# Reordering the first batch of an attention-plus-SwiGLU kernel: quarters of k and v, early dummy products, split copies, narrow first weights

## Chip, cores, metric

One core of one Trainium2 chip. The metric is device time in microseconds, the median of several executions. Other kernels were always timed beside runs of the kernel before, in the same rounds on the same chip. All runs quoted are of the fast state, and every run gave correct results.

A word on the spread: executions of the kernel before lie between 580.8 and 583.1 us, one at 584.2. The trace's span is some 1.8 us shorter than the time (581.1 for 582.86).

## The reference

```python
k_proj = einsum('ks,bhsd->bhkd', E, k)          # E, F: 64 x 1024
v_proj = einsum('ks,bhsd->bhkd', F, v)          # q, k, v: 8 x 8 x 1024 x 64
attn   = softmax(q @ k_proj^T / 8)              # over 64 columns
x      = (attn @ v_proj) -> (8192, 512)
out    = (silu(x @ w_gate) * (x @ w_val)) @ w_out   # 512 -> 1536 -> 512
```

Inputs and output are float32; the kernel computes in bf16 with float32 sums.

## The kernel before

The kernel is one long stream of products for 16 chunks of 512 tokens: gate, value, then output, with the attention of the next batches placed between them. Only batch 0 has no stream to hide in. These are the parts of its start that the argument touches:

```python
def u_KV(b, what="kv", hs=(0, H), at="a"):      # project heads hs of k and/or v
    t = ...one PSUM bank, [128, 8, 64] f32...
    for j in range(8):                           # 8 products per call and operand
        matmul(out=t[lo:lo+64, h0:h1], lhsT=w[:, j], rhs=src[b][:, h0:h1, j], ...)
    if "k" in what: scalar.copy(ks[:, h0:h1], t[0:64, h0:h1])
    if "v" in what: vector.tensor_copy(BDV[0:64, ps, 0:64], ...); vector.tensor_copy(BDV[64:128, ps, 64:128], ...)

def u_KT(b, at="a"):                             # transpose k', spread it into block-diagonal BD
    ...4 transposes into one PSUM tile...
    for c in range(2):
        vector.tensor_copy(bd[0:64, :, c, 0:64], src)
        copy(scalar if b else vector, bd[64:128, :, c, 64:128], src)

# ... batch 0, in program order (cut):
turn(0); warm(4)                                 # E transposed; 4 dummy products
for h in range(7): cast_k(gpsimd if h == 3 else vector, h)
load_q(0, 0, 2); load_v(0, 2); load_w_gv(0); load_w_gv(1)     # 4 blocks of 128 columns
u_KV(0, "k", (0, 4), at="y"); warm(2)
cast_k(scalar, 7)
u_KV(0, "k", (4, 8), at="y")
turn(1)                                          # F transposed
u_KT(0, at="v")
# u_T: q transposed; u_S: scores and exp; u_R, u_N: row sums, scaling; u_A: A transposed; u_PV: A v'
u_T x4 and u_S x4
for u in range(3): u_R(0, u); u_N(0, u)
u_KV(0, "v", (0, 4), at="y"); u_R(0, 3); u_N(0, 3)
u_A(0, 0); warm(2); u_A(0, 1); u_KV(0, "v", (4, 8), at="y"); u_A(0, 2)
u_PV x2; u_A(0, 3); u_PV x2                      # then the stream: f_g, f_v, ...
```

The softmax here doesn't subtract the row's maximum and nothing guards it: scores larger than these inputs give would overflow.

## Time and profile before

| | before |
|---|---|
| median time | 581.71 us (580.81 to 582.29, 4 runs) |
| profiled run | 582.86 us, span 581.1 |
| TensorE busy | 98% |
| first scores / first value group begin | 16.68 / 26.52 us |
| span from there on | 554.56 us |

In a timeline line stand: start in us, duration, engine, source line, operation, written and read tiles, count, and in brackets how long the engine had been idle and what released it. "kvp" are the projections, "sc" the scores, "aTp" the transposes of A, "pv" A times v', "gps" and "vps" gate and value products. "PEld" are weight loads. BD and BDV are k' and v' spread into block-diagonal tiles; PSUM is the memory that TensorE writes its sums to, in banks. The beginning of the first value group is the marker of what follows. A warning on the clock column: it averages the records of the granted clock, and before the first record it says 1.00 although the durations show half speed. The profiled run of the kernel before has a mean of 1.000 although its first record comes at 20.92 us. I read the first rise from durations and from the time of that record.

### The profile page before, as it was taken

To read this page: it belongs to the slowest core of one execution; us is meant where nothing else is said; L and a number is where in the kernel's file an instruction comes from. 1 tells how busy PE (TensorE), PEld (TensorE's weight loads), DVE (VectorE), ACT (ScalarE), POOL (GpSimd) and SP (SyncE) were. 2 spreads that over 40 slices of the span, in tenths; PEclk is the share of its full clock that TensorE was granted. 3 is DMA by queue.
4 is the path that set the end of the run, shared out by engine and by line. 5 is a ranking of instruction groups with operands and counts; after the bars stand their busy time and mean duration, and the time that the engine had idled before them with its cause. 6 is when DMAs were issued, how large, how long until landed. Compare 5 with 4: busy or idle time off the path is not lost.

```text
span 581.1 us, 7901 instructions
## 1 busy us (share of the span) xinstructions
PE 567.6 (98%) x2952; PEld 268.1 (46%) x2952; DVE 337.7 (58%) x576; ACT 242.4 (42%) x428; POOL 106.8 (18%) x119
## 2 busy tenths in 40 slices
PE   5999999999999999999999999999999999999997
PEld 3644444544444444444444444444444444444443
DVE  2787564766556664666546764566555674545550
ACT  2545435454435434354345434354343533443321
POOL 5625040224102320025001240022300220000000
PEclk9999999999999999999999999999999999999999
DMA  9999955309930399016980289313990124001012
GB/s 223 190 200 192 205 87 100 73 19 170 203 81 37 80 194 179 37 45 110 177 159 29 63 145 197 74 38 77 183 193 37 38 55 73 37 36 37 19 37 91
DMA packets 100599, 61.34 MB, mean 106 GB/s; under 512 B 51792, under 2 KB 91216, under 8 KB 100560
## 3 DMA queue, kind: packets, MB, share of 16 engines
q0 software_dynamic: 40176, 28.84, 34.3%
q1 hardware_dynamic: 60384, 31.99, 23.9%
q8 instruction: 23, 0.38, 0.3%
q14 instruction: 16, 0.13, 0.1%
HBM read 60.29 MB, written 16.78 MB: 133 GB/s over the span
## 4 chain that ended last, share of the span: by engine, by line
PE 94%; ACT 2%; DVE 2%; DMA 1%; issue 0%; SPq 0%; DVEq 0%; ACTq 0%
PE yps L344 28%; PE vps L318 28%; PE gps L303 28%; PE kvp L150 3%; PE sc L229 3%; PE pv L287 2%; DMA kraw<-in_k_dram 1%; DVE hT L332 1%; PE qTp L195 1%; PE aTp L276 1%; ACT qT L138 0%; DVE s L327 0%; DVE zz L244 0%; PE kTp L174 0%; ACT ysb L353 0%
## 5 line engine op out<-in xcount | busy, mean ns | idle before, releaser
L327 DVE SCALAR_TENSOR_TENSOR s<-th,gps 128x512 f32<-128x512 f32 x192 | 130.5, 680 | 136.1 <-ACT th L311 135.8
L303 PE MATMUL gps<-xT,wg 128*128 128x512 bf16 x768 | 197.9, 379 | 0.5 <-ACT xT L138 0.3
L318 PE MATMUL vps<-xT,wv 128*128 128x512 bf16 x768 | 197.2, 379 | 0.0
L344 PE MATMUL yps<-wo,hT 128*128 128x512 bf16 x768 | 194.6, 379 | 0.7 <-ACT ysb L353 0.7
L311 ACT ACTIVATE th<-gps 128x512 f32<-128x512 f32 x192 | 114.7, 597 | 154.4 <-PE gps L303 152.7
L332 DVE TENSOR_TENSOR hT<-s,vps 128x512 bf16<-128x512 f32 x192 | 132.0, 688 | 22.8 <-PE vps L318 2.5
L344 PEld LDWEIGHTS <-hT 128*128 128x128 bf16 x768 | 75.1, 98 | 91.5 <-issue 1.0
L318 PEld LDWEIGHTS <-wv 128*128 128x128 bf16 x768 | 72.9, 98 | 83.4 <-issue 4.0
L303 PEld LDWEIGHTS <-wg 128*128 128x128 bf16 x768 | 73.1, 98 | 81.9 <-issue 1.0
L260 POOL TENSOR_TENSOR AAd<-ee,rr 128x512 bf16<-128x512 f32 x48 | 49.9, 1040 | 300.6 <-issue 165.3
L353 ACT ACTIVATE ysb<-yps 128x512 f32<-128x512 f32 x64 | 38.2, 597 | 76.0 <-PE yps L344 76.0
L138 ACT CAST xT<-pv 128x512 bf16<-128x512 f32 x61 | 35.4, 584 | 50.4 <-PE pv L287 50.4
L244 DVE TENSOR_REDUCE zz<-ee 128x8 f32<-128x512 f32 x64 | 43.5, 680 | 20.0 <-ACT ee L233 19.7
L233 ACT ACTIVATE ee<-sc 128x512 f32<-128x512 f32 x64 | 38.0, 597 | 20.0 <-PE sc L229 18.8
L260 POOL TENSOR_TENSOR AA<-ee,rr 128x512 bf16<-128x512 f32 x15 | 15.5, 1040 | 63.7 <-DVE rr L246 25.8
L287 PE MATMUL pv<-AT,BDV 128*128 128x512 bf16 x64 | 23.6, 379 | 0.9 <-ACT AT L138 0.7
L229 PEld LDWEIGHTS <-qTd 128*128 128x128 bf16 x192 | 14.8, 98 | 11.3
L150 PE MATMUL kvp<-kb,ET 128*64 128x512 bf16 (+1 forms) x72 | 17.1, 389 | 1.7 <-POOL kb L138 1.0
L229 PE MATMUL sc<-BD,qTd 128*128 128x128 bf16 x192 | 18.6, 219 | 0.0
L246 DVE RECIPROCAL rr<-zz 128x8 f32<-128x8 f32 x64 | 13.0, 203 | 6.3
L164 DVE CAST BDV<-kvp 64x256 bf16<-64x256 f32 (+1 forms) x9 | 3.6, 396 | 22.3 <-ACT ks L160 20.0
L150 PE MATMUL kvp<-vb,FT 128*64 128x512 bf16 (+1 forms) x72 | 16.4, 375 | 0.0
(50 smaller groups left out, 157.1 us busy)
## 6 DMA issues: line engine op xcount, KB each, us to landing
out_dram<-ysb SPq DMA_DIRECT2D x64, 256.0 KB, 2.3
qb<-in_q_dram POOLq DMA_DIRECT2D x15, 512.0 KB, 17.2
kb<-in_k_dram POOLq DMA_DIRECT2D x7, 1024.0 KB, 11.5
vb<-in_v_dram POOLq DMA_DIRECT2D x7, 1024.0 KB, 14.0
kraw<-in_k_dram SPq DMA_DIRECT2D x4, 512.0 KB, 6.0
wg<-in_moe_w_gate_dram POOLq DMA_DIRECT2D x6, 256.0 KB, 10.2
wv<-in_moe_w_val_dram POOLq DMA_DIRECT2D x6, 256.0 KB, 10.7
wo<-in_moe_w_out_dram POOLq DMA_DIRECT2D x2, 768.0 KB, 15.4
```

The lines of the kernel that those rows point to most:

```text
L150: nc.tensor.matmul(out=t[lo : lo + 64, h0:h1].rearrange("p h d -> p (h d)"), lhsT=w[:, j, :], rhs=src[b][:, h0:h1, j, :], start=(j == 0), ...
L229: nc.tensor.matmul(out=ps[:, n, :], lhsT=t[:, n, :], rhs=BD[b % 2][:, 4 * g + n, :], start=True, stop=True)
L233: nc.scalar.activation(out=e[:].rearrange("p h j k -> p (h j k)"), in_=ps[:].rearrange("p a k -> p (a k)"), func=AF.Exp, scale=scale,)
L244: nc.vector.reduce_sum(out=z[:], in_=e[:], axis=AX.X)
L260: eng.tensor_tensor(out=a.rearrange("p j h k -> p h j k"), in0=ee.pop((b, u))[:], in1=rr.pop((b, u))[:].unsqueeze(3).to_broadcast([P, 4, 2 ...
L303: nc.tensor.matmul(out=ps[:], lhsT=wg[:, kt, f * P : (f + 1) * P], rhs=x[:, kt, :], start=(kt == 0), stop=(kt == NKT - 1),)
L311: nc.scalar.activation(out=th[:], in_=ps[:], func=AF.Tanh, scale=0.5)
L318: nc.tensor.matmul(out=ps[:], lhsT=wv[:, kt, f * P : (f + 1) * P], rhs=x[:, kt, :], start=(kt == 0), stop=(kt == NKT - 1),)
L327: nc.vector.scalar_tensor_tensor(out=s1[:], in0=th[:], scalar=1.0, in1=g[:], op0=ALU.add, op1=ALU.mult)
L332: nc.vector.tensor_tensor(out=hT[c][:, f, :], in0=s1[:], in1=ps[:], op=ALU.mult)
L344: nc.tensor.matmul(out=yy[c][:], lhsT=hT[c][:, f, i * P : (i + 1) * P], rhs=wo[:, f, :], start=(f == 0), stop=(f == NFT - 1),)
L353: nc.scalar.activation(out=ysb[:], in_=yy.pop(c)[:], func=AF.Copy, scale=0.5)
```

## The change

The intent: start the stream sooner. Project k and v by quarters as they land, cast k on three engines, turn k' in two halves with its copies split over VectorE and ScalarE, let dummy products open TensorE's clock from the beginning, take F's turn out of the way of the scores, begin row sums early, and load only one block of 128 weight columns ahead of the softmax.

```diff
-            nc.vector.tensor_copy(out=BDV[b % 2][0:64, ps, 0:64], in_=tv[:, ps, 0, :])
+            copy(nc.vector if b else nc.scalar, BDV[b % 2][0:64, ps, 0:64], tv[:, ps, 0, :])
...                                   # u_KT, now for prs=(0, 2) and (2, 4)
-            copy(nc.scalar if b else nc.vector, bd[64:128, :, c, 64:128], src)
+            nc.scalar.copy(out=bd[64:128, slice(*prs), c, 64:128], in_=src)
...
-        nc.sync.dma_start(out=ef[1][:], in_=F)
+        zeros = const.tile([P, CW], BF16, name="zeros"); nc.vector.memset(zeros[:], 0.0)
...
+        warm(8)
         turn(0)
-        warm(4)
-        for h in range(7): cast_k(nc.gpsimd if h == 3 else nc.vector, h)
+        warm(6)
+        cast_k(nc.vector, 0); cast_k(nc.gpsimd, 1)
         load_q(0, 0, 2)
-        load_v(0, 2); load_w_gv(0); load_w_gv(1)
+        load_v(0, (0, 4, 6, 8)); load_w_gv(0, 1)
+        cast_k(nc.vector, 2); cast_k(nc.scalar, 3)
+        nc.scalar.dma_start(out=ef[1][:], in_=F)
+        u_KV(0, "k", (0, 2), at="y"); u_KV(0, "k", (2, 4), at="y")
+        cast_k(nc.vector, 4); cast_k(nc.scalar, 5)
+        warm(2)
+        u_KV(0, "k", (4, 6), at="y"); u_KT(0, at="v", prs=(0, 2))
+        cast_k(nc.vector, 6); cast_k(nc.scalar, 7)
+        warm(2)
+        u_KV(0, "k", (6, 8), at="y"); u_KT(0, at="v", prs=(2, 4))
...                                   # T0, T1, S0, S1, R0, N0, then turn(1), T2, T3, ...
+        load_w_gv(1, 2) ... load_k(1)            # the other loads, behind the row scaling
+        warm(3)
+        u_A(0, 0, nc.scalar); u_A(0, 1, nc.scalar); u_KV(0, "v", (0, 4), at="y"); u_A(0, 2, nc.scalar)
+        u_PV(0, 0, 0, nc.vector); u_A(0, 3, nc.vector); u_PV(0, 0, 1, nc.scalar)
+        u_KV(0, "v", (4, 6), at="y"); u_PV(0, 0, 2, nc.vector)
+        u_KV(0, "v", (6, 8), at="y"); u_PV(0, 0, 3, nc.scalar)
```

## The prediction

> **What bounds the kernel now.** I read the page first, then busy times by stretch, then the timeline of the start, then the DMA view.
>
> ```profile
> PE 567.6 (98%) x2952; PEld 268.1 (46%) x2952; DVE 337.7 (58%) x576; ACT 242.4 (42%) x428; POOL 106.8 (18%) x119
> PE   5999999999999999999999999999999999999997
> ```
>
> TensorE bounds the span; only the first and last slices (14.5 us each) are not full. By stretch (length, then PE, PEld, DVE, ACT, POOL busy, clock, DMA share, GB/s):
>
> ```profile
> 0.00:5.00 5.00, 0.42 (x4) 0.45 (x5) 1.51 (x4) 1.28 (x1) 1.14 (x8) 1.00 0.58 161
> ...
> 100.00:560.00 460.00, 460.00 (x2352) 214.41 (x2350) 273.41 (x457) 194.01 (x341) 71.52 (x72) 1.00 0.50 92
> ```
>
> From 100 to 560 us PE is never idle. The change touches only the first batch, so its worth is how much sooner the dense stream of gate and value products begins. The timeline shows that start, with its waits:
>
> ```profile
> 4.58 1.11 PE L431 MATMUL efp<-ident_fp,Eraw 64*128 64x64 f32 x8 [4.58 <-DMA Eraw<-in_E_dram]
> ...
> 11.47 0.62 ACT L138 CAST kb<-kraw 128x512 bf16<-128x512 f32 x1 [0.63 <-DMA kraw<-in_k_dram]
> ...
> 12.14 1.87 PE L150 MATMUL kvp<-kb,ET 128*64 128x256 bf16 x8 [0.73 <-ACT kb L138]
> ...
> 13.94 1.14 PE L431 MATMUL efp<-ident_fp,Fraw 64*128 64x64 f32 x8
> ...
> 16.42 0.29 DVE L138 COPY BD<-kTp 64x256 bf16<-64x256 bf16 x1
> ...
> 16.68 0.61 PE L229 MATMUL sc<-BD,qT 128*128 128x128 bf16 x4
> ...
> 18.93 1.92 PE L150 MATMUL kvp<-vb,FT 128*64 128x256 bf16 x8
> ...
> 21.81 1.06 PE L150 MATMUL kvp<-vb,FT 128*64 128x256 bf16 x8
> ...
> 24.93 0.59 PE L287 MATMUL pv<-AT,BDV 128*128 128x512 bf16 x2 [0.67 <-ACT AT L138]
> ...
> 26.52 1.02 PE L318 MATMUL vps<-xT,wv 128*128 128x512 bf16 x4
> ```
>
> The first value group starts at 26.52; that is my marker. The path to it: last k quarter lands at 11.4; cast; eight products (1.87); F's eight transposes (1.1); k' transposed; four copies of k' into BD one after another on DVE (15.50 to 16.71); scores from 16.68; softmax, A transposes, PV; marker. Two stretches, then: 16.68 to the scores, 9.84 from there.
>
> The DMA view of the first 13 us:
>
> ```profile
> GB/s 0 0 0 0 0 0 151 252 233 239 290 183 208 384 384 391 372 347 359 372 391 391 384 403 397 391 378 422 378 120 107 77 93 176 195 191 173 183 189 180
> kraw<-in_k_dram SPq DMA_DIRECT2D x4, 512.0 KB, 6.0
> qb<-in_q_dram POOLq DMA_DIRECT2D x2, 256.0 KB, 4.9
> ```
>
> k streams at 370 to 400 GB/s until about 9.5, then a hole of some 1.5 us before q and v flow, because POOL issued q only at 8.47, after its cast of head 3. (Casting transfers are counted by the bytes written, so 190 there is some 380 read.) Dividing the same view into single issues gives landings of k at 5.7, 7.6, 8.9 and 11.4, q 13.2 and 14.5, v 18.2 and 20.7, first weights 22.0 and 23.4. All land before they are used, so in the second stretch no transfer is the bound.
>
> **What the Trainium skill says.** "TensorE: Matmul & The Clock Gate", Part 1: the array runs at half clock until it has been busy through a free-running window of about 3.4 us. The trace agrees: eight like products took 1.92 us at 18.93 and 1.06 at 21.81, so TensorE was cold for 20 us, its gaps breaking every window. "Perfetto Trace Analysis", DVE / Act Engine Instruction: the sequencer pushes an instruction into a wait queue and fetches the next. So F's DMA, though written after a cast on ACT, may be issued early. ACT issues no DMA here, so this trace can't show it. "DMA: Bandwidth & Descriptors", Specifications: line rate needs 512 bytes or more. The new 128-column weights are written as 256-byte rows; no row here shows their rate.
>
> **The change part by part.**
>
> (1) Dummies from a zero tile. A DVE memset of this size takes 0.27 (the BDV ones); DVE starts at 0.91, so PE starts near 1.25 instead of 4.58. Eight cold products at 0.43 (two took 1.04 with overlap, four 1.86) run to 4.7, E's turn to 5.8, six more to 7.5 or 8.4. Some 6 us are dense, so a full window fits and the clock should be full by about 8. The dummies lie in dead time: first casts end at 6.4.
>
> (2) k by quarters, casts shared by DVE, ACT and POOL. A quarter is eight products of 128 columns: 1.87/2 = 0.94 cold, about 0.5 warm. But ACT now does four things in strict order: cast 3, ks copies, cast 5, ks copy, two BD copies, cast 7. With 0.62 per cast and 0.25 (estimate, from 0.36 for double the size) per small copy: cast 3 at 7.6 to 8.25, two ks to 9.0, cast 5 to 9.9 (k at 8.9, slowed by F and q), products, ks to 10.75, BD copies to 11.3, cast 7 to 11.9 or 12.1. So it is no earlier than now, when it ends at 12.09. After it: products 0.5 (saves 1.4), ks 0.3, no F turn (saves 1.1), k' transposes 0.3, half of the BD copies on two engines 0.5 (saves 0.7). With q in place (two qT copies, 0.6 side by side) scores start near 14.1 instead of 16.68: 2.6 gained.
>
> (3) Second stretch, from scores at 14.1. ACT: exp 0, 1 to 15.65; F's half 0.4; qT 2, 3 to 17.2 (0.58 each, both now on ACT and behind the exps); exp 2, 3 to 18.35. Now all four exps ended 3.08 after the first scores; then 4.25. Row sums: N0 on POOL 16.0 to 17.05, N1 to 18.25, N2 18.7 to 19.75, N3 on DVE 19.55 to 20.25. A0, A1, v(0:4) are done by 19.75; A2 to 20.1; BDV copy on DVE behind N3 to 20.55; PV0 20.6; xT0 on DVE 20.95 to 21.65; A3's copy on DVE behind it to 22.1; v(4:6) and its copies to 22.3; PV2 22.35, xT2 to 23.4; v(6:8) 22.6 to 23.1, copies to 23.6; PV3 23.65; xT3 on ACT 24.05 to 24.65; last gate product 24.7; value group near 24.9. That is 10.8 against 9.84: 1.0 given back.
>
> (4) Loads. POOL is free after one cast at 6.55, so q goes out 1.9 us earlier and the hole fills; v should land by 18. The 128-column pair is in by 20 or 21. The next pairs go out behind N2, from 19.8, landing from about 24 on; each column block of 128 needs 0.52 MB at 380 GB/s = 1.4 us against 1.73 us of products, so the stream keeps ahead. Nothing on the path.
>
> Sum: 2.6 - 1.0 = 1.6 us; 581.7 - 1.6 = 580.1.
>
> **Rivals.**
> (a) The clock stays cold, because F32 transposes or gaps break the window again. For: it was cold through 20 us that the page calls nearly all busy. Quarters then cost 0.94 and every later PE step doubles; I estimate 1 to 1.3 us back: 581.2.
> (b) The k path isn't held by casts but by landing. With POOL and ACT issuing q and F into k's stream, the last quarter could land at 12 or later, and nearly half of the front gain goes: 580.9. Against: by 8.4 nearly all of k has moved.
> (c) The tail isn't as serial as I laid it: with warm products and DVE and ACT both free, the second stretch takes 9 us as the author meant, marker at 23, 578.2. Against: xT0, A3 and N3 share DVE, and PV2 stands ahead of v(6:8) in PE's order.
> (d) Weights come late, since three of the first four 128-column blocks are now issued behind the softmax instead of ahead of it: a stall of 1 to 2 us around 26 to 29 eats the gain: 581.7. Against: the margins in (4) are over 1 us.
>
> **Range and chances.** The path from 1.25 to 24.9 is some forty steps, each uncertain by some 0.1, with two open switches (clock, landing), and repeats of before spread over 1.5 us. I put 8 in 10 on 578.2 to 581.5, centre 580.1. Even a marker at 17 would not give 11.6 us, and the start can't lose that, so within 2% is all but sure: 0.98, with 0.01 each side.
>
> **What would show it.** Right: PE busy from about 1.3; the eight v products in about 1 us instead of 1.92; scores near 14; first value group near 25; same length from there to the end; PE busy without waits on weights. Step 2 is wrong if cast 7 waits for k rather than for ACT's order; step 3 is wrong if the marker comes less than 10 us after the first scores, or more than 11.5; the whole is wrong if the time moves without the marker moving.

## The result, and the profile after

The changed kernel took 586.46 us (586.03 to 587.28, 4 runs) against 581.71: slower by 0.85 per cent. Ratios are the mean time of one kernel's fast runs over the mean of the other's of the same rounds, so not quite the ratio of the medians; here 1.0085, 95% interval 1.0067 to 1.0103.

The page of the changed kernel, busy times, then TensorE by slice of 14.6 us and its granted clock:

```profile
PE 571.6 (98%) x2989; PEld 268.9 (46%) x2989; DVE 336.6 (58%) x575; ACT 245.3 (42%) x438; POOL 108.7 (19%) x122
PE   7799999999999999999999999999999999999997
PEclk9799999999999999999999999999999999999999
```

The second slice has a clock of 7 tenths: something new. The timeline of the start, the lines that answer to those shown of before:

```profile
1.19 3.59 PE L442 MATMUL warm<-zeros 128*128 128x512 bf16 x8 [1.19 <-DVE zeros L414]
...
7.72 0.62 ACT L137 CAST kb<-kraw 128x512 bf16<-128x512 f32 x1 [1.90 <-DMA kraw<-in_k_dram]
...
7.73 0.54 ACTq L458 DMA_DIRECT2D Fraw<-in_F_dram  x1
...
14.33 0.61 PE L149 MATMUL kvp<-kb,ET 128*64 128x128 bf16 x8 [1.25 <-ACT kb L137]
...
17.24 1.03 PE L228 MATMUL sc<-BD,qT 128*128 128x128 bf16 x8 [1.21 <-ACT qT L137]
...
30.10 1.02 PE L317 MATMUL vps<-xT,wv 128*128 128x512 bf16 x4
```

First scores at 17.24 instead of 16.68; first value group at 30.10 instead of 26.52. After it the span goes on for 585.06 - 30.10 = 554.96 us, against 554.56. So nearly the whole loss lies ahead of the marker: 0.56 us up to the scores, 3.02 between scores and marker, 0.4 behind it.

What fills this time is in the chain of waits, followed back from the first value group of the changed kernel (start, us, what):

```profile
6.37 2.72 PE warm L442 x6
9.09 0.87 PE kvp L149 x8
...
9.98 0.27 ACT ks L159
...
10.29 0.62 PE kvp L149 x8
...
12.57 0.23 DVE BD L181
...
12.82 0.27 ACT BD L182
...
13.11 0.24 DVE BD L181
...
13.37 0.26 ACT BD L182
...
13.66 0.63 ACT kb L137
...
21.66 1.28 PE warm L442 x3
22.94 0.69 PE aTp L275 x8
...
24.66 0.27 ACT BDV L137
...
24.95 0.31 DVE BDV L137
```

Three things stand here that I had put beside the path. Dummies: six of them run until the first products of k, three until the A transposes. Products that wait for a copy: the second quarter waits until ScalarE has taken the first out of the same bank. And copies in turns: DVE, ACT, DVE, ACT, one after the other. Behind those four copies stands the cast of the last head, behind that the last quarter of k.

### The profile page after: what moved, and what is told of

It reads as the page before. It is cut to its first block, busy times and chain, and to the rows that moved or that the text cites. A ratio compares the mean times of both kernels' runs of the same rounds, so it can differ in the third digit from the quotient of the medians.

```text
span 585.1 us, 7989 instructions
## 1 busy us (share of the span) xinstructions
PE 571.6 (98%) x2989; PEld 268.9 (46%) x2989; DVE 336.6 (58%) x575; ACT 245.3 (42%) x438; POOL 108.7 (19%) x122
## 4 chain that ended last, share of the span: by engine, by line
PE 94%; ACT 2%; DVE 2%; issue 1%; DVEq 0%; ACTq 0%
PE yps L343 28%; PE vps L317 28%; PE gps L302 27%; PE kvp L149 3%; PE sc L228 3%; PE pv L286 2%; PE warm L442 1%; DVE hT L331 1%; ACT qT L137 1%; PE aTp L275 0%; PE efp L430 0%; PE qTp L194 0%; DVE s L326 0%; ACT BD L182 0%; DVE zz L243 0%
## 5 line engine op out<-in xcount | busy, mean ns | idle before, releaser
L259 POOL TENSOR_TENSOR AA<-ee,rr 128x512 bf16<-128x512 f32 x15 | 15.6, 1040 | 66.0 <-ACT th L310 27.7
L228 PEld LDWEIGHTS <-qTd 128*128 128x128 bf16 x192 | 14.7, 98 | 11.3
L137 DVE CAST BDV<-kvp 64x256 bf16<-64x256 f32 (+2 forms) x17 | 6.7, 396 | 22.9 <-ACT ks L159 20.0
L149 PE MATMUL kvp<-vb,FT 128*64 128x512 bf16 (+2 forms) x80 | 15.7, 339 | 0.0
## 6 DMA issues: line engine op xcount, KB each, us to landing
kb<-in_k_dram POOLq DMA_DIRECT2D x7, 1024.0 KB, 11.3
```

Of the source, the lines that this page charges most:

```text
L137: (nc.scalar.copy if eng is nc.scalar else eng.tensor_copy)(out=out, in_=in_)
L149: nc.tensor.matmul(out=t[lo : lo + 64, h0:h1].rearrange("p h d -> p (h d)"), lhsT=w[:, j, :], rhs=src[b][:, h0:h1, j, :], start=(j == 0), ...
L228: nc.tensor.matmul(out=ps[:, n, :], lhsT=t[:, n, :], rhs=BD[b % 2][:, 4 * g + n, :], start=True, stop=True)
L259: eng.tensor_tensor(out=a.rearrange("p j h k -> p h j k"), in0=ee.pop((b, u))[:], in1=rr.pop((b, u))[:].unsqueeze(3).to_broadcast([P, 4, 2 ...
```

## The experiments

Each line of the table is one kernel. First scores and first value group are from its profiled run and depend on when that run's clock rose, so only runs with the same rise are to be compared closely (changed, e3, e7: 9.6 to 9.7 us; e1, e8: 10.1 to 10.2; e4, e12, e13, e14: 5.4 to 5.9; the others 3.9 to 5.3). The clock is the range of the mean granted clock over the timed runs.

What the rise alone is worth can be read from e10 and e5, which have the instructions of the changed kernel up to the scores, but for the loads of weights (e10) and one more transposed part of q (e5). From the timeline of e10, whose clock rose at 5.1:

```profile
6.32 1.46 PE L442 MATMUL warm<-zeros 128*128 128x512 bf16 x6 [0.52 <-DVE ET L137]
...
12.72 0.61 PE L149 MATMUL kvp<-kb,ET 128*64 128x128 bf16 x8 [1.25 <-ACT kb L137]
...
15.64 1.03 PE L228 MATMUL sc<-BD,qT 128*128 128x128 bf16 x8 [1.21 <-ACT qT L137]
```

The scores begin at 15.64 in both, 1.60 us sooner than in the profiled run of the changed kernel: that much of its 17.24 is the late rise. How often its other runs rose late the record does not show. The profiled runs of e3 and e7, with the same late rise, were the slowest of theirs, so there the trace shows less than the median gained.

| kernel | median | before | ratio (95%) | scores | value group | clock |
|---|---|---|---|---|---|---|
| changed | 586.46 | 581.71 | 1.0085 (1.0067-1.0103) | 17.24 | 30.10 | 0.993-0.994 |
| e1 fewer dummies | 585.62 | 581.92 | 1.0062 (1.0049-1.0074) | 15.60 | 27.62 | 0.987-0.999 |
| e2 one engine per tile | 585.22 | 581.92 | 1.0057 (1.0043-1.0071) | 14.41 | 27.85 | 0.993-1.000 |
| e3 v ahead | 584.81 | 581.92 | 1.0047 (1.0034-1.0061) | 17.27 | 29.26 | 0.993-0.994 |
| e4 before + dummies | 581.78 | 581.92 | 1.0000 (0.9988-1.0013) | 15.25 | 25.28 | 0.994-1.000 |
| e5 second stretch as before | 584.66 | 582.25 | 1.0042 (1.0026-1.0059) | 15.64 | 26.13 | 0.991-0.997 |
| e6 casts ahead | 584.50 | 582.25 | 1.0044 (1.0030-1.0059) | 14.75 | 26.31 | 0.994-1.000 |
| e7 gaps filled | 583.95 | 582.25 | 1.0038 (1.0026-1.0050) | 17.20 | 28.75 | 0.999-1.000 |
| e8 rebuilt | 581.71 | 582.25 | 0.9988 (0.9976-1.0000) | 14.15 | 23.77 | 0.993-0.999 |
| e9 rebuilt, filled | 581.34 | 581.82 | 0.9993 (0.9981-1.0005) | 14.84 | 24.88 | 0.996-1.000 |
| e10 weights early | 586.24 | 581.82 | 1.0076 (1.0063-1.0090) | 15.64 | 28.68 | 0.993-0.994 |
| e11 three repairs | 583.47 | 581.82 | 1.0029 (1.0017-1.0041) | 15.65 | 26.83 | 1.000 |
| e12 four repairs | 583.18 | 581.97 | 1.0020 (1.0001-1.0040) | 14.49 | 24.31 | 0.999-1.000 |
| e13 rebuilt, filled otherwise | 580.48 | 581.97 | 0.9974 (0.9957-0.9991) | 13.91 | 23.53 | 0.996-1.000 |
| e14 five repairs | 581.32 | 582.20 | 0.9991 (0.9977-1.0004) | 14.62 | 25.04 | 0.999-1.000 |

My theory after reading the trace: a serial chain of hand-overs (dummies, copies in turns, quarters) and, beside it, a clock that falls in the gaps. The rivals: only the clock; only the new order of the second stretch; the weights, which come late.

### e1: dummies on the path?

```diff
         turn(0)
-        warm(6)
...
-        warm(3)
         u_A(0, 0, nc.scalar)
```

> The changed kernel without two of its five rows of dummy products (the six after E's turn, the three ahead of the A transposes). Theory 'dummies on the path': the changed kernel's chain of waits has 2.72 + 1.28 us of them where real operands are ready, so about 2 us come back (some k copies wait for the landing of k anyway), 584.4 us, with the first value group near 28. Rival 'the clock pays for them': without them the array turns to full speed only after 17 us or later, every product of the first stretch takes twice as long, and the time is the same or longer, 586.5 to 588.

Measured: 585.62, ratio 1.0062; 0.23 per cent, 1.3 us, back. In the profiled run the first products of k start as soon as their operand is cast, and the A transposes right behind the scores, at 19.39 (timeline):

```profile
6.79 1.03 PE L149 MATMUL kvp<-kb,ET 128*64 128x128 bf16 x8 [0.94 <-DVE kb L137]
```

That is 6.79 instead of 9.02, and the value group comes at 27.62 instead of 30.10. The median gained only half of that. The dummies stood on the path, but what they cost depends on the clock: in e10 the six took 1.46 us and not 2.72, and its scores, with the dummies in place, came at 15.64 against 15.60 here. That the dummies also fed the clock is not shown: two runs of e1 had a mean of 0.993 and one 0.987, the lowest of all, but that one took 585.31, while the slowest, 586.19, had 0.999. The expectation was met in direction, not in size.

### e2: one engine for each PSUM tile

```diff
-            copy(nc.vector if b else nc.scalar, BDV[b % 2][0:64, ps, 0:64], tv[:, ps, 0, :])
+            copy(nc.vector, BDV[b % 2][0:64, ps, 0:64], tv[:, ps, 0, :])
...
-            nc.scalar.copy(out=bd[64:128, slice(*prs), c, 64:128], in_=src)
+            copy(nc.scalar if b else nc.vector, bd[64:128, slice(*prs), c, 64:128], src)
```

> The changed kernel with the block copies of k' and of v of the first batch all on VectorE, none on ScalarE. Theory 'two engines on one PSUM tile take turns': the four copies last as long as before (about 1 us for each half), but ScalarE is free and its cast of the eighth head comes 1 us sooner; scores 0.4 to 0.7 us sooner, 585.9 us. Rival 'the split works and the order is elsewhere at fault': the copies on one engine take twice as long, scores 0.5 us later, 587 us.

Measured: 585.22, ratio 1.0057, 0.28 per cent back, more than I expected. The timeline of the changed kernel shows two of the four copies, with what each waited for; that of e2 shows the same copies on one engine:

```profile
12.82 0.26 ACT L182 COPY BD<-kTp 64x128 bf16<-64x128 bf16 x1 [0.15 <-DVE BD L181]
13.11 0.23 DVE L181 COPY BD<-kTp 64x128 bf16<-64x128 bf16 x1 [0.32 <-ACT BD L182]
```

```profile
11.01 0.22 DVE L137 COPY BD<-kTp 64x128 bf16<-64x128 bf16 x1
11.24 0.23 DVE L181 COPY BD<-kTp 64x128 bf16<-64x128 bf16 x1
```

On two engines four copies lasted from 12.57 to 13.63, 1.06 us; on VectorE alone from 10.78 to 11.71, 0.93. Splitting gained nothing and cost a hand-over each time (0.03 us from the end of one copy to the start of the other engine's); it also kept ScalarE from its cast. From the first products of k to the scores e2 takes 6.90 us (7.51 to 14.41) where e10, with nearly the same rise, takes 7.93 (7.71 to 15.64): 1.0 us sooner, where I had expected 0.4 to 0.7. The Trainium skill says why two readers may not simply overlap: "PSUM — Partial Sum Buffer", Terms, has it that two engines on the same bank and the same 32 partitions at once is a collision, reads against reads included. In each pair of copies both engines read the same 64 partitions of one tile, and the trace agrees: each copy began after the other's end. (Between the two halves of the partitions the rule would allow an overlap; the program as built makes none. So that rule alone does not account for all the turns. Nor does writing into one tile force them: VectorE and ScalarE cast two heads of k into the one tile kb at once, both from 7.72.) I had not looked that page up.

### e3: v ahead of the tail

```diff
-        warm(3)
+        u_KV(0, "v", (0, 4), at="y")
         u_A(0, 0, nc.scalar)
         u_A(0, 1, nc.scalar)
-        u_KV(0, "v", (0, 4), at="y")
+        u_KV(0, "v", (4, 8), at="y")
...
-        u_KV(0, "v", (4, 6), at="y")
...
-        u_KV(0, "v", (6, 8), at="y")
```

> The changed kernel with v's first half projected in place of the last three dummies and its second half, whole, in the old place of the first: no quarters in the tail. Theory 'tail of quarters': from the end of the last row scaling to the first value group 5.6 us shrink to about 4, 584.8 us. Rival 'the tail is bound by the order of the xT and A copies on VectorE': the tail stays over 5 us, 586 us.

Measured: 584.81, ratio 1.0047, 0.38 per cent back at the same clock and the same scores (17.27): the tail is a part of the loss by itself. From the last row scaling's end to the value group: 24.50 to 30.10, 5.6 us, became 24.52 to 29.26, 4.7. I had expected 4. These 0.8 us are less than half of the 0.38 per cent (2.2 us). What was left is in the timeline of e3:

```profile
24.91 1.03 PE L149 MATMUL kvp<-vb,FT 128*64 128x256 bf16 x8 [0.83 <-DVE BDV L137]
```

v's second half waits for VectorE's copy of the first half, and that stands behind the row scaling in VectorE's order.

### e4: the dummies alone, in the kernel before

```diff
+        zeros = const.tile([P, CW], BF16, name="zeros"); nc.vector.memset(zeros[:], 0.0)
...                                   # the dummies read zeros
+        warm(8)
         turn(0)
```

> The kernel before with a zero tile and eight dummy products from 1.2 us on, nothing else. Theory 'an early clock is worth little because it drops again in the gaps': first value group within 0.5 us of 26.5, 581 to 582 us. Rival 'the early clock is the part of the change that pays': the second half of k (1.87) and the first of v (1.92) at full speed, first scores 1 us sooner, 580 us.

Measured: 581.78 against 581.92, ratio 1.0000. In the profiled run the clock rose at 5.9 us and stayed, scores came at 15.25 and the value group at 25.28, outside the 0.5 us of the theory; yet its time, 581.60, is no better than usual for the kernel before. So the profiled run of before, with its clock up only at 20.9 us, was one of its slower ones: 582.86 where the median is 581.71. Between these two profiled runs the early clock is worth 1.24 us at the marker and 1.26 in time. That the dummies gain nothing in the median is measured; that most runs of the kernel before rise early without them would explain it, but is not shown.

### e5: the second stretch in the order of before

```diff
-        (T0, T1, S0, S1, R0, N0, turn(1), T2, T3, ... quarters of v ...)
+        u_T(0, 0..2); u_S(0, 0); u_T(0, 3); u_S(0, 1..3); R, N for 0..2
+        turn(1)
+        ... v in halves, A, PV as in the kernel before; later weights last
```

> The changed kernel up to k', then the second stretch in the order of the kernel before (F turned after the scores, v projected in halves beside the softmax, later weights issued last). Theory 'the second stretch lost 3 us of the 4 to 5': from first scores to first value group 9.8 us instead of 12.9, 584 us or a little less. Rival 'the front lost it, and the second stretch is only a victim of the low clock': still over 12 us, 586 us.

Measured: 584.66, ratio 1.0042, 0.43 per cent back. From scores to value group 26.13 - 15.64 = 10.49 us instead of 12.86 (13.04 in e10, with the same scores), though the clock fell there too (15.6 to 19.0). The order of the second stretch is a part of the loss. In this version what follows the value group took 555.61, 0.65 more than in the changed kernel: a first sign of the weights (TensorE's weight loads waited 0.44 and 0.83 us for their landing), see e12.

### e6: casts ahead in ScalarE's order

```diff
+        cast_k(nc.vector, 4); cast_k(nc.scalar, 5)
         u_KV(0, "k", (0, 2), at="y"); u_KV(0, "k", (2, 4), at="y")
-        cast_k(nc.vector, 4); cast_k(nc.scalar, 5)
+        cast_k(nc.vector, 6); cast_k(nc.scalar, 7)
         warm(2)
         u_KV(0, "k", (4, 6), at="y"); u_KT(0, at="v", prs=(0, 2))
-        cast_k(nc.vector, 6); cast_k(nc.scalar, 7)
```

> The changed kernel with the casts of k's third and fourth quarter put ahead of the copies of the quarters before in ScalarE's order. Theory 'ScalarE's order holds the last quarter': its products start at about 12.6 us instead of 14.3, first scores 1.7 us sooner, 584.8 us. Rival 'the dummies ahead of the first products hold everything': under 0.5 us gained, 586 us.

Measured: 584.50, ratio 1.0044, 0.41 per cent back. The timeline of e6:

```profile
11.80 0.63 PE L149 MATMUL kvp<-kb,ET 128*64 128x128 bf16 x8
```

The last quarter's products start at 11.80 instead of 14.33, but most of that is the earlier rise: in e10 they start at 12.72. From the first products of k to the scores e6 takes 7.20 us (7.55 to 14.75), e10 7.93. So ScalarE's order is worth 0.7 us up to the scores, less than half of the 1.7 expected. The runs of this version also had a better clock (0.994 to 1.000); how much of the median's gain is order and how much clock stays open.

### e7: the gaps filled, nothing else moved

```diff
-        warm(2)
+        warm(7)
         u_KV(0, "k", (6, 8), at="y")
...
         u_T(0, 1, "a", nc.vector)
+        warm(5)
         u_S(0, 0, "g")
```

> The changed kernel with five more dummies in each of the two gaps of over 1.2 us ahead of the scores. Theory 'the clock falls because TensorE waits': it stays full from about 10 us on, the two score rows, F's turn and the A transposes take half as long, 585 us. Rival 'the dummies stand on the path': where they run at half clock they take 2.1 us and not 1.1, 587 us.

Measured: 583.95, ratio 1.0038: 0.47 per cent back, by the means the largest of the single repairs (the intervals of e5, e6 and e7 overlap), by adding ten useless products. Busy times of the stretch in which the changed kernel's clock was up, and of the next, in which it was down (length, PE, PEld, DVE, ACT, POOL, clock, DMA share, GB/s), first of the changed kernel, then of e7:

```profile
9.67:16.50 6.83, 4.22 (x44) 2.68 (x42) 1.40 (x6) 3.12 (x10) 1.76 (x3) 1.00 1.28 210
16.50:23.30 6.80, 5.81 (x41) 4.26 (x42) 3.72 (x9) 4.25 (x9) 2.47 (x3) 0.50 0.69 89
```

```profile
9.67:16.50 6.83, 5.76 (x53) 3.46 (x52) 1.45 (x6) 3.18 (x10) 1.80 (x3) 1.00 1.30 216
16.50:23.30 6.80, 5.98 (x58) 4.13 (x56) 4.45 (x11) 5.46 (x12) 3.40 (x4) 1.00 0.63 78
```

In the changed kernel TensorE was busy for 4.22 of 6.83 us (1.49 of the last 3.42, which hold the first gap and part of the second) and then had half the clock for 6.8 us. In e7 it was busy for 5.76 (3.03 of the last 3.42) and kept it. The two profiled runs are alike up to there (rise at 9.7 and 9.6, scores at 17.24 and 17.20), so their value groups, 30.10 and 28.75, measure the fall of the clock: 1.35 us, half of what the median gained. All timed runs of the changed kernel had a mean clock of 0.993 or 0.994, all of e7 0.999 or more. Even with the clock held, scores to value group take 11.55 us (11.56 in e6, whose clock held too), 1.7 more than before and 1.5 more than the 10.03 of e4, whose clock was up: the clock is one part, the order the other.

### e8, e9, e13: a version from these findings

```diff
-        warm(6)
+        warm(4)
...                                   # casts 0 to 7 ahead of the copies, k in halves:
+        u_KV(0, "k", (0, 4), at="y")
+        cast_k(nc.vector, 6); cast_k(nc.scalar, 7)
+        warm(3); u_KT(0, at="v", prs=(0, 2))
+        u_KV(0, "k", (4, 8), at="y")
+        warm(1); u_KT(0, at="v", prs=(2, 4))
+        u_T(0, 0..2); u_S(0, 0); u_T(0, 3); u_S(0, 1..3)
+        for u in range(4): u_R(0, u); u_N(0, u)
+        turn(1)                       # both copies of F on ScalarE
+        u_A(0, 0, nc.scalar); u_KV(0, "v", (0, 4), at="y")
+        u_A(0, 1, nc.scalar); u_KV(0, "v", (4, 8), at="y")
+        u_A(0, 2, nc.vector); u_PV(0, 0, 0, nc.vector); u_A(0, 3, nc.scalar)
+        u_PV(0, 0, 1, nc.scalar); u_PV(0, 0, 2, nc.vector); u_PV(0, 0, 3, nc.scalar)
...                                   # 4 blocks of weights ahead of the softmax, as before
...                                   # BD copies on VectorE; BDV: first half ScalarE, second VectorE
```

> A version from what has been seen: dummies only where TensorE has nothing to do, k in halves, each PSUM tile emptied by one engine, casts ahead of copies, F turned after the scores, row sums in one row, v projected ahead of the tail. If the steps of the argument hold: first scores at 13.5 to 15, first value group at 22 to 24, 578 to 580 us, faster than both. If the low clock or something not seen rules, it stays at 581 to 583 us.

Measured: 581.71, ratio 0.9988 (0.9976 to 1.0000). The marker is early (23.77 in the profiled run, 580.09 us), but the four other runs, all at a mean clock of 0.993 or 0.994, took 581.4 to 582.0: the median lies in the range of the rival. So I filled its gaps:

> The rebuilt version with nine more dummies in the gaps where its TensorE waited. Four of the five runs of the rebuilt version had a mean granted clock of 0.993 and took 581.4 to 582.0, one had 0.999 and took 580.1. Theory 'the fall of the clock costs 1.5 us': all runs at 0.998 or more, 579.5 to 580.5. Rival 'the spread has another cause, or the dummies stand on the path': 581 to 582 as before.

Measured: 581.34, ratio 0.9993. The clock was at 0.996 to 1.000, the time was not: a miss. The profiled run of e9 had its clock at half from 7.9 to 11.3, ahead of most of the fillers, and three runs at 1.000 took 580.62 to 581.66. The timeline of e9 shows one thing that these dummies cost:

```profile
17.91 1.02 PE L442 MATMUL warm<-zeros 128*128 128x512 bf16 x4 [0.52 <-ACT FT L137]
18.77 0.39 PE L275 MATMUL aTp<-ident_bf,AA 128*128 128x128 bf16 x4
```

The dummies write to a PSUM bank that F's copy has to leave first, then run in front of the A transposes. e13 has fewer, and puts those after F's turn into a bank that the scores have left:

```diff
-        warm(1); u_KT(0, at="v", prs=(2, 4))
+        warm(2); u_KT(0, at="v", prs=(2, 4))
...
+        warm(2)                       # between u_T(0, 1) and u_T(0, 2)
...
         turn(1)
+        warm(3, "g")
```

> The rebuilt version with dummies in its gaps, but the ones after F's turn in a bank that the scores have left, so that they wait for nothing and end ahead of the first A transpose; in the version before they waited for F's copy and held the A transposes back by 0.9 us. If the clock is what four of five runs of the rebuilt version lost, all runs are at 0.998 or more and take 580 to 580.8 us. If not, 581.3 to 582 us.

Measured: 580.48, ratio 0.9974 (0.9957 to 0.9991): faster than both kernels, by a quarter of a per cent over the one before. Its marker in the timeline:

```profile
23.53 1.02 PE L317 MATMUL vps<-xT,wv 128*128 128x512 bf16 x4
```

Its interval overlaps those of e8 and e9, so that the fillers made this difference is likely, not shown. The median was as forecast, the clock was not: three of the six runs had 0.996 to 0.997 and yet took 580.45 to 580.87, and the slowest, 581.74, had 1.000. So the mean clock does not account for the spread of these versions.

### e10: weights early, nothing else

```diff
-        load_w_gv(0, 1)
+        load_w_gv(0, 2); load_w_gv(2, 4)
...
-        load_w_gv(1, 2); load_w_gv(2, 4)
```

> The changed kernel with the first four 128-column blocks of weights issued ahead of the softmax again, as in the kernel before. Theory 'the weights are off the path': the hole in the transfers at 20 to 25 us goes, the time stays within 0.5 us of the changed kernel's, 586 to 587. Rival 'late weights hold the stream': 585 or less.

Measured: 586.24, ratio 1.0076 where the changed kernel had 1.0085; the intervals overlap. The transfers' hole from 20 to 25 us is filled (135 GB/s there instead of 1), the time is not moved. In the changed kernel the weights are off the path.

### e11, e12, e14: the repairs added up

e11 has e3, e6 and dummies in its gaps (five after the first quarter's products, five ahead of the scores; not the same ten as in e7). e12 also has the copies of k' on VectorE alone, v's first half on ScalarE and its second on VectorE; e14 has e10's loads besides.

> The changed kernel with the three single repairs that gained most (casts ahead, gaps filled, v ahead of the tail) together. Each alone took off 0.38 to 0.47 per cent. If they act on different stretches they add to 1.2 per cent, 579 to 580 us; if they overlap, as I expect because a held clock shortens what the others move, 581 to 582.5 us.

Measured: 583.47, ratio 1.0029. Alone the three took back 0.38 + 0.41 + 0.47 = 1.26 per cent; together 0.56. They overlap, and the time missed even the range that I gave for this. v's second half again waited for VectorE, 1.67 us. Hence:

> The three repairs together, and each PSUM tile of k' and v emptied by one engine. With three repairs the second half of v waited 1.67 us for VectorE's copy of the first half, which stood behind the last row scaling; and the scores waited for four copies in turns. If splitting copies over two engines is the fourth part of the loss, v's second half starts without that wait, the first value group comes 1.3 to 1.8 us sooner, 581.7 to 582.2 us, level with the kernel before. If the rest is in the order of the second stretch (F's turn, late qT copies), under 0.6 us is gained, 583 us.

Measured: 583.18, ratio 1.0020, less than expected, although the value group came at 24.31. What follows it took 555.90 us. The waits of TensorE between 24 and 36 us of e12 (in us, times, longest):

```profile
PE gps L302 <- DMA wg<-in_moe_w_gate_dram: 0.7, 1, 0.7
PE vps L317 <- DMA wv<-in_moe_w_val_dram: 0.3, 1, 0.3
```

TensorE now waits for weights: once the rest was repaired, the loads behind the softmax came onto the path. So:

> The four repairs and the first four blocks of weights issued ahead of the softmax. With four repairs the first value group came at 24.3 us, but the second and third gate and value groups then waited 0.72 and 0.28 us for weights, and what follows the first value group took 555.9 us instead of 554.6. If the weights are now the bound, the time falls by about 1.3 us to 581.5 to 582, level with the kernel before. If not, 583.

Measured: 581.32 against 582.20, ratio 0.9991 (0.9977 to 1.0004): level with the kernel before, and 554.55 us from the value group on, with no wait for weights. With five repairs the loss of 0.85 per cent is undone. The same load order that was worth nothing in e10 was worth 0.29 per cent here by the means, though the intervals of e12 and e14 still touch; the waits for weights, 1.0 us in e12 and none in e14, bear it out.

## Why the prediction was wrong, point by point

The forecast was 580.1; measured 586.46, 6.4 us more. The trace splits that: scores 3.1 us later than forecast, second stretch 2.1 longer, 0.4 behind the marker, which make 5.6; and 0.8 because the profiled run that I read was 1.15 us above its kernel's median, while that of the changed kernel was 0.37 above.

The steps that failed are the dead time of the dummies in step 1, the copies "on two engines 0.5" in step 2, and the 10.8 us of step 3, with a fall of the clock that no step had.

- Step 1, TensorE from 1.25 us: right, 1.19. "The dummies lie in dead time" is where it first failed: the six after E's turn waited for a bank (to 6.37) and then ran to 9.09 at half clock, while the first operands were ready at 6.65. I had noted "7.5 or 8.4" for their end and did not carry it on to the quarter behind them. The clock was full at 9.7 in this profiled run, not 8 (at 5.1 in e10, where they ended at 7.7), and fell again at 16.5.
- Step 2, scores at 14.1: measured 17.24. 1.60 of the miss is the late rise, since e10 and e5 had them at 15.64; the other 1.5 is the step's own. The mechanism, cast 7 behind ScalarE's order and not behind k's landing, was right: k had landed by 10.4 us (issued up to 3.0, at most 7.4 to landing), and the cast began at 13.66. The sizes were not: in e10 the cast ended at 12.67, not 11.9 to 12.1, and from there to the scores it took 2.97 us, not 2.0 to 2.2. The term mis-sized: BD copies "half ... on two engines 0.5" took 1.06, because they take turns (e2), and that twice, once ahead of the cast, once ahead of the scores. Besides, the second quarter waited 0.35 for the copy of the first.
- Step 3, 10.8 us from scores to marker: measured 12.86, and so wrong by its own sign (over 11.5). 1.31 of it is the fall of the clock (e7). Without it 11.55: the three dummies ahead of the A transposes, which my list of the stretch left out, and copies of v in turns; how these 0.75 us divide was not measured. The direction, that the second stretch gives time back, was right; the amount was three times the 1.0 that I gave.
- Step 4, weights off the path: right for this kernel (e10), but with a thinner margin than I said. The second pair of blocks was issued at 23.89, not 19.8, and in e12 they were the bound.
- Rival (a), the clock, was real, but not as I had it: the clock rose, late in the profiled run (1.60 us at the scores), and then fell. That its 1 to 1.3 us fit the 1.35 of e7 is luck. I had given it as an alternative; it came on top. Rival (b), k's landing, did not occur. Rival (c), a less serial tail, was wrong: the tail was more serial. Rival (d) was wrong here and came true in e12.
- Two readings were off. "Its gaps breaking every window" is not what the trace shows: from 14.09 to 17.51 TensorE was busy for 3.40 of 3.42 us, and the clock rose only at 20.92. And k's stream ran at 347 to 422 GB/s, not 370 to 400, which changes no sum.
- The range: I had treated some forty steps as if their errors were independent and equally likely to either side. But each unforeseen wait only adds. The forecast that the time stays within 2 per cent held.

What stays open: why the medians of e3 and e7 gained more than their traces show, and what decides whether the clock rises or falls. The changed kernel lost it after a stretch with TensorE busy for 62 per cent; e4's profiled run kept it at 66 and 67 per cent (6.62 of 10.10 and 5.34 of 8.00 us), but another run of e4 had a mean of 0.994. In shorter stretches it is no clearer: e1 kept its clock through 2.04 of 3.41 us busy and lost it after the next, 2.09 of 3.41; e9 lost it after 2.27 of 3.41. A limit can't be read from these.

## What to carry to other kernels

Cutting a start-up into smaller pieces paid here only where the pieces run side by side: in these programs two engines emptying one PSUM tile, or a product writing to a bank that is being emptied, took turns, and each turn is a hand-over. Dummy products are instructions in TensorE's order like any other: look where their operands' bank comes free and what stands behind them. And when a loss has several causes, single undoings overlap and one cause can hide behind another, so add the repairs up until the time is level.

## What the Trainium skill lacked or had wrong

- "TensorE: Matmul & The Clock Gate", Part 1, gives in its table of the two states the way back to half clock as at least one idle window of about 3.4 us; a later passage on clocks that swing allows for short idles, without a size. Here the clock fell at 16.5 us with no gap of TensorE over 1.25 us, after 4.22 busy of 6.83 (1.49 of the last 3.42), and stayed down for 6.8 us although 5.81 of 6.80 were busy.
- "Perfetto Trace Analysis", DVE / Act Engine Instruction, lets the sequencer go on once an instruction is in the wait queue. F's transfer on ScalarE's queue, which came next after a waiting cast, was issued at 7.73 when the cast began at 7.72; at 7.07 and 7.07 in e1, 7.35 and 7.34 in e2. In these programs it did not go ahead. Whether the cast's wait was an instruction of its own the trace does not show.
- No page that I read says what it costs when two engines take turns at small copies: here 1.06 us for four of 64 x 128 elements in turns against 0.93 on one engine, with 0.03 us from one engine's end to the other's start; nor what a product waits whose bank is being emptied, here 0.35 us.
